# Evacuations of the projections and transposes raised in priority, the seeds' work on g one slot later

## The chip, the cores and the metric

The kernel runs on one core of a Trainium2 chip. A core has a matrix engine (PE, with its weight loads listed as PEld), a vector engine (DVE), an activation engine (ACT), a general engine (POOL) and a sync engine (SP) that here only issues DMA transfers. Each engine executes its own instruction list strictly in order and waits on semaphores for the others. The metric is the device time of one execution in microseconds (us), as the median of several runs.

## The reference

Two independent halves, joined on the last axis. The first is a state-space convolution over 2048 positions and 448 channels with 256 complex states per channel; the second is a 16-head softmax attention over 2048 positions, 28 values per head.

```python
A = -jnp.exp(log_A_real) + 1j * A_imag
C = (C_real + 1j * C_imag) * dt[:, None]
P = jnp.exp((A * dt[:, None])[:, :, None] * pos[None, None, :])
K = 2.0 * jnp.einsum("dn,dnl->dl", C, P).real
y = irfft(rfft(u) * rfft(K)) + u * D_skip

q, k, v = split(x @ wqkv)
o = softmax(q @ k.T * scale) @ v
b = o @ wo
return concatenate([y, b], axis=-1)
```

## The kernel before

The kernel has an opening and a main loop. In the opening, x is transposed on PE and multiplied with the split weights (48 projection jobs, 12 matmuls each); the results go to DRAM and are read back in the layout that attention needs. Next to that the "seeds" of the convolution are computed: eight groups `o` of channels, each of which produces the powers and phases (tiles `tri`, `sg`, `qhat`) from which the main loop later builds the kernel K. In the main loop the scores, exponentials and products with v run on PE and ACT, and the convolution fills the other engines. At the end of the opening the row maxima of the first query block are computed (tiles `p` and `rl`, 16 rounds), negated into `mh`, and sent by two small DMAs into `qhat`; the first score matmul (`pss`) waits for these.

What sets the order of the work differs between the two parts. In the main loop the instructions stay in the order in which the code issues them. In the opening a scheduler orders each engine's list: every instruction carries a priority that follows from the place at which the code issues it, and of those that it takes to be ready, the scheduler puts the one with the earliest place first. A buffer is given out again when the instructions that use it are done.

The opening's code is written in slots. `slots[t]` holds the seeds' steps that fall into slot t, and `project()` is called between slots so that the 48 jobs spread over the first 37 of 41 slots. A seeds group o starts its step list at slot 4·o; the steps are named in the list that `seeds` returns. Those that matter here:

- `times_dt` and `exp_a` (ACT, tile `nat`) prepare a group's inputs; `turn` transposes them on PE into a PSUM tile `pn` (8 matmuls `pn<-ident,nat`) and copies one part on ACT (`tr`).
- `phases` multiplies on POOL (`tri<-tr,pw`) and on DVE (`tri<-pn,pw` and two more of 1680 elements, the last of them in `reduce`).
- `sines` and `sizes` are ACT work on `tri` and `sg` with sine and exponential tables; a change between these needs a table load (`ACT_TABLE_LOAD`).
- `factors`, `g_base` and `e_all` are POOL multiplications (`sg<-sg`, `tri<-tri`, `qhat<-tri`); `g_base` also has a copy of 224 elements on ACT.
- `g_first` is nine DVE operations on `sg` and a PSUM tile `px` of which there is one; `g_copies` is four ACT copies (`sg<-pn`, `sg<-px`); `put_e` and `put_g` are the stores of `qhat` and `sg`.

A job's result is a PSUM tile `pm`, of which there are three. The next use of a `pm` tile waits for the evacuation of the job three before. The evacuation of a K or Q job is an ACT copy and a DVE subtraction into `hl` (two buffers, stored by DMA), for some K jobs also `kb` and `dhl`; that of a V job one ACT copy into `v`. `project()` issues the matmuls of one job and then the evacuation of the job before, which waits in the list `pend`. `transposes(c)` does the same for x: four PE transposes into `pt`, one ACT copy `xh`, one DVE subtraction `xl`.

When the opening's PSUM pools are closed, four `p` tiles of two banks each take over all eight banks: the first two tiles lie over the `pm` banks and one `pt`, the next two over the other `pt`, the two `pn` and `px`. In the code order, all seeds' steps stand ahead of the maxima.

All helpers record through line 76, so the profile shows line 76 everywhere and the tile names tell what an instruction is. In this document job n is the n-th projection job (0 to 47; 40 to 47 are the last K and Q jobs), and a tile with a number, such as `pn6` or `sg7`, is that tile of seeds group 6 or 7 (0 to 7).

Of the kernel before, what the change touches and what calls it, by code (L numbers as in the profile page):

```python
# [8 lines left out]
F32 = mybir.dt.float32  # L9
F32R = mybir.dt.float32r  # L10
I32 = mybir.dt.int32
AF = mybir.ActivationFunctionType
ALU = mybir.AluOpType
# [28 lines left out]
SGB, XB, XL = 2, 5, 4  # L42
K0, KP, KD, UP = 0, 3.5, 4, 3
A0, A1, KW = 26, 34, (33, 35, 36)

N1 = 32
N2 = 64
# [44 lines left out]
def body(ctx, tc, a, out):  # L92
    nc = Engines(tc)
# [119 lines left out]
    with ExitStack() as st:  # L213
# [100 lines left out]
        def seeds(o):  # L314
# [105 lines left out]
            put_e = lambda: nc.sync.dma_start(sd_d[o][:, :, :F_G].rearrange("b p f -> p b f"), q["se"])  # L420
            put_g = lambda: nc.sync.dma_start(sd_d[o][:, :, F_G:].rearrange("b p f -> p b f"), q["sg"])

            def load():
                if o not in nats:
# [1 line left out]
                q["nat"] = nats.pop(o)  # L426
            dts = lambda *r: [lambda i=i: times_dt(i) for i in r]
            return [[load], dts(1, 2, 3), [], [exp_a] + dts(0), [turn, phases], [g_place, reduce], [sines], [sizes, places, g_base],
                    [e_all, g_first], [put_e, factors], [g_copies], [], [put_g]]

        xh, xl = {}, {}

        def transposes(c):
            for k in range(NCK):
                pt = ps_t.tile([128, CQ], F32, name="pt")[:CK]
                for t in range(4):
                    nc.tensor.transpose(pt[:, t * 128:(t + 1) * 128], xns[c, t // 2][:, t % 2, k * CK:(k + 1) * CK], ident)
                xh[k] = x_p.tile([CK, CQ], F32R, name="xh", bufs=XB)
                xl[k] = x_p.tile([CK, CQ], F32R, name="xl", bufs=XL)
                nc.scalar.activation(xh[k], pt, AF.Copy)  # L440
                nc.vector.tensor_tensor(xl[k], pt, xh[k].bitcast(F32), ALU.subtract)

        def qk_proj(c, s, g):
            pp = w_tile()
# [46 lines left out]
        for c in range(NQ):  # L491
            jobs = [lambda c=c, s=s, g=g: qk_proj(c, s, g) for g in range(G) for s in (1, 0)]
            v_jobs = [lambda c=c, t=t: v_proj(c, t) for t in range(4)]
            jobs = v_jobs + jobs if c == NQ - 1 else jobs + v_jobs
            jobs[0] = (lambda c, f: lambda: (transposes(c), f())[1])(c, jobs[0])
            if c + 1 < NQ:
                jobs[1] = (lambda c, f: lambda: (load_x(c + 1), f())[1])(c, jobs[1])
            work += jobs
        stages = [seeds(o) for o in range(NO)]
        n_stage = SP * (NO - 1) + len(stages[0])  # L500
        slots = [[] for _ in range(n_stage)]
# [4 lines left out]
        pend, n_work = [], len(work)  # L506
# [10 lines left out]
        def project():  # L517

            e = work.pop(0)() if work else None
            while pend:  # L520
                pend.pop(0)()
            if e:
                pend.append(e)

        for t in range(n_stage):
            while work and n_work - len(work) < n_work * (t + 1) / PW:
                project()
            for f in slots[t] + ahead.get(t, []):
                f()
            if t + 1 == PW:  # L530
                project()
                wst.close()
                load_k(0, HG - 1, k0_p)
                load_q(1)
                for c in range(NQ):
                    load_v(0, c)
# [211 lines left out]
    def fin(u, s_):  # L748
# [15 lines left out]
        def scale():  # L764
            pw = w_tile()
            for t in range(4):
                nc.tensor.transpose(pw[:, t * 128:(t + 1) * 128], rb[:, t].rearrange("p h e -> p (h e)"), ident)
            nc.vector.tensor_tensor(on, o, pw, ALU.mult)
            if g < G - 1:
                nc.sync.dma_start(on_d[c][g], on)  # L770
            else:
                p_due.extend((s_ + PD + PS * t, lambda t=t: project(t)) for t in range(4))
# [385 lines left out]
```

## Time and profile before

| | |
|---|---|
| median of 3 runs | 1303.45 us (1303.38 to 1304.3) |
| the profiled execution, its own time | 1307.74 us |
| its span | 1305.7 us |
| first score matmul `pss` in it | 242.89 us after the span's start |
| PE busy over the span | 1228.7 us (94%) |
| ACT, DVE, POOL busy over the span | 980.3, 907.0 and 865.9 us |

The page splits the span into 40 slices of 32.6 us; the opening is the first seven and a half. There PE's row reads 6, 8 and 7 tenths, behind it mostly 9. A row of a timeline reads: start, duration, engine, line, operation, output<-inputs, shapes, count, and in brackets how long the engine sat idle before it and what ended the wait. A row of waits reads: who waited for whom, us in total, times, longest. The chain of waits is followed back from the end of a stretch, step by step, to what released each instruction.

### The profile page before, as it was taken

The numbers are of one execution on the slowest core, as the hardware profiler recorded it, in microseconds if no ns is written. First come the engines' busy times: TensorE is split into PE (matmuls) and PEld (weight loads), VectorE is DVE, ScalarE is ACT, GpSimd is POOL, SyncE is SP. The second block draws the span as 40 slices with busy tenths as digits, with TensorE's granted clock in tenths as the row PEclk, the third lists the DMA queues.
The fourth block names the chain that finished last, engine by engine and source line by source line (L and its number), as shares of the span: only waits on it lengthen the run. The fifth ranks groups of instructions, "written<-read, shape, count | busy, mean of one in ns | idle before, by whom it ended". The sixth has DMA issues, their size and how long they took to land.

```text
span 1305.7 us, 32148 instructions
## 1 busy us (share of the span) xinstructions
PE 1228.7 (94%) x12193; PEld 695.7 (53%) x12193; DVE 907.0 (69%) x2001; ACT 980.3 (75%) x2046; POOL 865.9 (66%) x684
## 2 busy tenths in 40 slices
PE   6888877799999999999999999999997999999998
PEld 5766755355555555555555555555554555545333
DVE  5676656677777787777788888888986555636111
ACT  4877875588888888888788888888886666756463
POOL 2677654478888788888769999999995221424421
PEclk9989887799999999999999999999999999999999
DMA  6677679735866455468634232743324453647666
GB/s 202 207 273 257 218 259 271 212 66 136 185 147 142 109 149 157 142 169 231 162 104 105 56 83 62 157 111 78 82 59 139 146 158 136 203 142 238 202 161 175
DMA packets 200082, 205.28 MB, mean 157 GB/s; under 512 B 95992, under 2 KB 158520, under 8 KB 197880
## 3 DMA queue, kind: packets, MB, share of 16 engines
q1 hardware_dynamic: 199864, 203.22, 56.1%
q8 instruction: 96, 1.57, 0.5%
q14 instruction: 58, 0.48, 0.1%
q10 hardware_dynamic: 64, 0.02, 0.0%
HBM read 120.74 MB, written 82.18 MB: 155 GB/s over the span
## 4 chain that ended last, share of the span: by engine, by line
PE 72%; POOL 8%; ACT 7%; DVE 5%; DMA 4%; issue 4%; SPq 0%; ACTq 0%; POOLq 0%
PE pm L76 39%; PE pss L76 16%; PE po L76 16%; POOL sg L76 2%; POOL e L76 2%; DMA khat<-k 2%; POOL tri L76 2%; ACT tri L76 1%; ACT sg L76 1%; DVE mx L76 1%; POOL p L76 1%; ACT L76 1%; ACT p L76 1%; POOL eu L76 1%; DVE rl L76 1%
## 5 line engine op out<-in xcount | busy, mean ns | idle before, releaser
L76 ACT ACTIVATE p<-pss 128x512 f32<-128x512 f32 x1024 | 560.4, 609 | 109.9 <-PE pss L76 105.9
L76 PE MATMUL pss<-qhat,khat 128*128 128x512 f32 x1024 | 405.7, 402 | 4.0 <-DMA qhat<-mh 2.2
L76 DVE TENSOR_REDUCE mx<-pm 128x1 f32<-128x512 f32 x480 | 308.3, 683 | 121.2 <-PE pm L76 119.5
L76 PE MATMUL pm<-khat,qhat 128*128 128x512 f32 x720 | 314.4, 437 | 6.1 <-ACT rl L76 3.5
L76 POOL TENSOR_TENSOR e<-e,sdb 128x256 f32<-128x256 f32 x168 | 202.0, 1203 | 108.7 <-ACT e L76 67.2
L76 PE MATMUL po<-p,v 128*32 128x512 f32 x2048 | 271.0, 597 | 0.0
L76 POOL TENSOR_TENSOR e<-e,eu 128x256 f32<-128x256 f32 x168 | 248.3, 1478 | 13.2
L76 PEld LDWEIGHTS pm<-khat,qhat 128*128 128x128 f32 x720 | 135.4, 188 | 206.4 <-ACT p L76 47.0
L76 PEld LDWEIGHTS pss<-qhat,khat 128*128 128x128 f32 x1024 | 191.2, 189 | 52.5 <-ACT p L76 13.8
L76 DVE CUSTOM_DVE_ANT_0 rl<-pm,rl 128x512 f32<-128x512 f32 x240 | 165.3, 689 | 70.0 <-ACT rl L76 67.7
L76 POOL TENSOR_TENSOR eu<-e,sdb 128x256 f32<-128x256 f32 x168 | 202.3, 1204 | 0.0
L76 POOL TENSOR_TENSOR p<-pr,pr 64x448 f32<-64x448 f32 x64 | 73.2, 1144 | 155.6 <-PE pm L76 122.3
L76 DVE TENSOR_TENSOR g<-g,zg 128x128 f32<-128x128 f32 x392 | 162.0, 413 | 3.6
L76 ACT ACTIVATE rl<-pm 128x512 f32<-128x512 f32 x240 | 145.3, 605 | 7.7 <-issue 4.1
L76 PE MATMUL pm<-xh,khat 112*128 112x512 f32 x256 | 89.7, 431 | 19.6 <-DVE hl L76 10.6
L76 PE MATMUL pm<-kdif,qhat 128*128 128x512 f32 x240 | 97.0, 404 | 1.7 <-DVE pr L76 1.1
L76 DVE TENSOR_TENSOR zg<-g,zg 128x128 f32<-128x128 f32 x224 | 88.0, 393 | 5.3
L76 PEld LDWEIGHTS pm<-e,g 128*32 128x32 f32 x3584 | 56.9, 110 | 49.2 <-issue 15.7
L76 PE MATMUL pm<-e,g 128*32 128x64 f32 x3584 | 73.6, 223 | 8.7 <-POOL e L76 8.7
L76 ACT ACTIVATE y<-pm 128x448 f32<-128x448 f32 x48 | 26.5, 553 | 59.7 <-PE pm L76 39.1
L76 PEld LDWEIGHTS pm<-xh,khat 112*128 112x128 f32 x256 | 51.0, 205 | 35.9 <-DVE hl L76 12.6
L76 DVE TENSOR_TENSOR pr<-pm,ub 128x448 f32<-128x448 f32 x64 | 37.0, 619 | 46.9 <-PE pm L76 37.7
(133 smaller groups left out, 1491.6 us busy)
## 6 DMA issues: line engine op xcount, KB each, us to landing
sdb<-sd SPq DMA_DIRECT2D x56, 336.0 KB
khat<-k SPq DMA_DIRECT2D x64, 256.0 KB
qhat<-q SPq DMA_DIRECT2D x64, 256.0 KB
sd<-sg SPq DMA_DIRECT2D x8, 1456.0 KB
k<-hl SPq DMA_DIRECT2D x16, 512.0 KB
q<-hl SPq DMA_DIRECT2D x16, 512.0 KB
v<-v SPq DMA_DIRECT2D x32, 256.0 KB
mw<-in_mw SPq DMA_DIRECT2D x16, 512.0 KB
```

Of the source, the lines that this page charges most:

```text
L76: i = f(*args, **kw)
```

## The change

Three places are edited, all in the opening.

```diff
+PRI = 200
...
             return [[load], dts(1, 2, 3), [], [exp_a] + dts(0), [turn, phases], [g_place, reduce], [sines], [sizes, places, g_base],
-                    [e_all, g_first], [put_e, factors], [g_copies], [], [put_g]]
+                    [e_all], [put_e, factors, g_first], [], [g_copies], [put_g]]
...
-                nc.scalar.activation(xh[k], pt, AF.Copy)
-                nc.vector.tensor_tensor(xl[k], pt, xh[k].bitcast(F32), ALU.subtract)
+                with tc.high_priority(offset=PRI):
+                    nc.scalar.activation(xh[k], pt, AF.Copy)
+                    nc.vector.tensor_tensor(xl[k], pt, xh[k].bitcast(F32), ALU.subtract)
...
-            while pend:
-                pend.pop(0)()
+            with tc.high_priority(offset=PRI):
+                while pend:
+                    pend.pop(0)()
```

Within `tc.high_priority(offset=PRI)` an instruction is ranked as if it had been issued 200 places earlier. This covers the evacuations of all 48 jobs with the DMA stores that they issue, and the two evacuation steps of all 16 x tiles. The seeds' `g_first` moves from step 8 to step 9 of a group's list and `g_copies` from step 10 to step 11. `put_g` stays in step 12, so that its slot is the old one. No instruction is added or removed: the lists of the engines hold the same instructions before and after, in another order up to the maxima of the first block, and in the same order from there on.

## The prediction

> **What bounds the kernel now.** The change reorders the opening alone, so I read the opening, from the chain of waits that ends at the first score matmul. Of it (start, duration, what):
>
> ```profile
> 200.78 0.63 POOL tri L76
> ...
> 205.06 0.56 DVE sg L76
> ...
> 205.80 0.40 ACT sg L76
> ...
> 206.69 0.76 DVE hl L76
> ...
> 218.32 10.46 DMA khat<-k
> ...
> 236.38 5.56 DMA qhat<-mh
> 242.00 2.99 DMA sdb<-sd
> ```
>
> The seeds' last group finishes its copies at 206.2 (I call this the seeds' end), the last K evacuation follows at 206.69, the khat loads wait for that evacuation's store in SP's list, the maxima wait for khat, and `mh` takes 5.56 us to land. PE's timeline gives the two instants that I measure by: the transposes `pn6` of group 6, and the first score.
>
> ```profile
> 159.05 0.71 PE L76 MATMUL pn<-ident,nat 56*128 56x56 f32 x8
> ...
> 242.89 0.77 PE L76 MATMUL pss<-qhat,khat 128*128 128x512 f32 x1 [2.18 <-DMA qhat<-mh]
> ```
>
> From 242.89 on PE is nearly saturated, and the main loop's order does not change. I therefore count each us by which the first score moves as one us of the total. Now PE's waits between 28 and 177 us, the stretch from job 4 to the start of job 44, and its work there (first pair behind the times: PE busy; then PEld, DVE, ACT, POOL, clock, DMA share, GB/s):
>
> ```profile
> PE pm L76 <- ACT v L76: 6.3, 5, 3.1
> PE pm L76 <- DVE hl L76: 6.2, 4, 2.0
> PE pm L76 <- DVE kb L76: 3.9, 3, 1.7
> PE pt L76 <- DVE xl L76: 1.9, 1, 1.9
> PE pm L76 <- ACT xh L76: 0.8, 1, 0.8
> ```
>
> ```profile
> 28.00:177.00 149.00, 129.85 (x590) 103.18 (x589) 101.67 (x149) 115.22 (x204) 98.12 (x68) 0.94 0.72 242
> ...
> 190.00:240.00 50.00, 34.20 (x111) 22.99 (x110) 27.51 (x50) 29.39 (x37) 15.50 (x12) 0.80 1.05 290
> ```
>
> All of PE's idle time there, 6.3 + 6.2 + 3.9 + 1.9 + 0.8 = 19.1 us, ends with an evacuation. These are exactly the instructions that are raised. The second window shows the DMA engines full from 190 to 240.
>
> **The change part by part.** Nothing is added or removed, 17 table loads included; what counts is which list position each thing gets. In the new lists an evacuation stands right behind its job on ACT and DVE. The seeds fall back against the jobs: `pn6` stood within job 38 on PE and now stands within job 44, behind 7 of its matmuls; `pn7` stood behind job 41 and now stands behind job 45. On ACT the last Q evacuation moves from the 254th to the 233rd place, while the last copy of group 7 moves only from the 252nd to the 254th. So the seeds' tail, from `pn6` to the seeds' end, now lies mostly behind the projections. I cost it in four steps.
>
> *When pn6 runs.* Before it PE has to do what it did up to 177, less the two `pn` groups (2 x 0.7 us), plus 7 matmuls of job 44 (about 1.6 us): 129.85 + 0.2 us of work from 28 us on, so 158.1 us if no idle time is left and 177.2 if all 19.1 us stay or are replaced. Replacement is possible: PE can now wait in the middle of a job for `nat`, which ACT prepares with lower rank, or for an `hl` buffer whose store has not landed. I take a quarter as left, 5 us, because every one of the five rows is of a raised instruction: 163. Both ends are kept.
>
> *From pn6 to the seeds' end.* The durations (count | us in total, mean ns of one):
>
> ```profile
> L76 ACT ACT_TABLE_LOAD x17 | 21.8, 1283 | 1.0 <-PEq L1148 0.7
> L76 ACT ACTIVATE tri<-tri 128x1008 f32<-128x1008 f32 x16 | 16.7, 1043 | 10.7 <-POOL tri L76 10.7
> L76 ACT ACTIVATE tri<-tri 128x1680 f32<-128x1680 f32 x8 | 12.8, 1604 | 0.0
> L76 ACT ACTIVATE sg<-tri 128x672 f32<-128x672 f32 x16 | 12.2, 764 | 3.8 <-POOL tri L76 3.7
> L76 ACT ACTIVATE hl<-pm,kones 128x512 fp32r<-128x512 f32 x16 | 10.9, 679 | 3.7 <-DMA k<-hl 2.4 <-PE pm L76 1.3
> L76 ACT ACTIVATE tri<-tri,half_pi 128x1008 f32<-128x1008 f32 x8 | 9.1, 1136 | 0.0
> L76 ACT ACTIVATE sg<-tri,half_pi 128x672 f32<-128x672 f32 x8 | 6.8, 853 | 0.0
> ```
>
> ```profile
> L76 POOL TENSOR_TENSOR qhat<-tri 128x784 f32<-128x784 f32 x16 | 29.8, 1869 | 0.0
> L76 POOL TENSOR_TENSOR sg<-sg 128x672 f32<-128x672 f32 x16 | 27.5, 1722 | 24.6 <-ACT sg L76 21.4 <-DVE pn L76 3.0
> L76 POOL TENSOR_TENSOR tri<-tr,pw 128x1680 f32<-128x1680 f32 x8 | 24.1, 3006 | 17.4 <-ACT tr L76 11.6 <-issue 5.8
> L76 POOL TENSOR_SCALAR sg<-sg 128x672 f32<-128x672 f32 x8 | 16.7, 2090 | 0.6
> L76 POOL TENSOR_TENSOR tri<-tri 128x224 f32<-128x224 f32 x16 | 10.7, 670 | 17.0 <-ACT tri L76 16.9
> ```
>
> I follow the new order from `pn6` at 0. POOL's 3.0 us product of group 6 ends at 4.2. ACT's exponential (1.04) and the last scaling for group 7 (about 0.5) end at 5.9; `pn7` runs; POOL's product of group 7 ends at 10.2. ACT: exponential of 7 to 11.3, two evacuations (about 0.65 each) to 12.6, table load to 13.9, sines of 6 (0.76 + 1.04) to 15.7, absolute value (about 1.5 net of overlap) to 17.2, cosine into `sg6` to 18.1, the last evacuation and the other cosine to 19.8. POOL in its order has one `sg6` product, a `tri6` and a 1.87 us `qhat6` ahead, until 18.9; then 1.72 + 2.09 + 0.67 to 23.4. The nine operations of `g_first` took from 201.4 (end of the first quoted chain row) to 205.6, 4.2 us; so to 27.6, and the copies, some 0.8, to 28.4. ACT is held by those copies, and only then does group 7: sine 0.76, load 1.28, exponential 0.76, absolute value 1.6, load 1.28, cosine 0.85, to 34.9. POOL 1.72 + 2.09 + 0.67 to 39.4, `g_first` to 43.6, copies to 44.4. Before it was 206.2 - 159.05 = 47.1 us, with six more evacuations and the waits that they brought in between. The seeds' end so falls at 163 + 44.4 = 207.4, about 1 us later than now.
>
> The Trainium skill bears on this step. DVE's last product of 1680 elements took 4.36 us once, beside a POOL product:
>
> ```profile
> 126.54 4.36 DVE L76 TENSOR_TENSOR tri<-tri 128x1680 f32<-128x1680 f32 x1
> ```
>
> ```profile
> 126.13 3.00 POOL L76 TENSOR_TENSOR tri<-tr,pw 128x1680 f32<-128x1680 f32 x1 [2.45 <-ACT tr L76]
> ```
>
> By the Trainium skill ("SBUF — State Buffer", Who interferes with whom), a DVE operation with two SBUF inputs and a GpSimd operation that reads SBUF shut each other out, and the second waits for the whole of the first; the trace agrees, since 1.9 us behind 129.13 is 131.0 and the row ends at 130.9. In the new tail that product of group 7 would meet POOL's group 6 products and push them back by some 1.9 us; by the rule my sum below would be 1298 instead of 1296.
>
> *From the seeds' end to the first score.* Now (rows of POOL, then of ACT):
>
> ```profile
> 207.42 5.86 POOL L76 TENSOR_SCALAR nq<-qhat 128x512 fp32r<-128x512 f32 x4 [2.16 <-DMA qhat<-q]
> ```
>
> ```profile
> 211.73 1.94 ACT L76 ACTIVATE rl<-p 128x1024 f32<-128x1024 f32 x2 [4.59 <-PE p L76]
> ...
> 229.66 2.18 ACT L76 ACTIVATE rl<-p 128x1024 f32<-128x1024 f32 x2 [1.82 <-PE p L76]
> ```
>
> The first `rl` came 5.5 us behind the seeds' end, because `nq` waited for a `qhat` load and PE for the last evacuation; and one round waited 1.82 us for khat. From the first `rl` to the issue of `mh` it took 236.38 - 211.73 = 24.65 us. After the change the last evacuation is some 24 us ahead of the seeds' end, so `qhat` and khat have landed. The first `rl` then waits for POOL, which has to finish the last `qhat` products (0.4 + 3.7 us behind 39.4) and one `nq` of 1.5 us: 1.4 us behind the seeds' end. Without the khat wait `mh` is issued 22.8 us later, at 231.6. The stores of group 7 no longer stand before it in the DMA engines; I take the 2.99 us of the `sdb` load as its landing, and 0.95 us from landing to the score as now (242.89 - 241.94): 235.5. If that cover fails, the old 5.56 costs 2.6 us more.
>
> *The DMA engines.* SP's list now has the khat loads behind the last Q store. Behind it stand 0.5 MB for that store, six `kdif` pieces of 0.06 MB, and by these rows 16 khat, 8 qhat and 2 `sg` stores of groups 5 and 6 and one of group 7; three v loads of 0.26 MB and two `qhat` stores of some 0.9 MB complete it.
>
> ```profile
> khat<-k SPq DMA_DIRECT2D x64, 256.0 KB
> qhat<-q SPq DMA_DIRECT2D x64, 256.0 KB
> ...
> sd<-sg SPq DMA_DIRECT2D x8, 1456.0 KB
> ```
>
> That is about 14 MB, at the 290 GB/s of the window 48 us. The Q store would go out at 163 + 20.5 = 183.5, so the DMA engines are done at 231.7, about when `mh` is issued. They set the same end, and bar a much earlier one.
>
> The moved `g_first` and `g_copies` cost nothing by themselves: their list places in the tail are in the walk above; without that cover each slot they move would cost one slot's work at most, some 4 us, once. Sum: 242.9 - 235.5 = 7.4 us less. The profiled execution's own time is 1307.74, 4.3 us above the median of 1303.45; I take the gain off the median: 1303.45 - 7.4 = 1296.0.
>
> **The rivals.** (1) *The seeds are held by PE* (slower). `pn6` and `pn7` now stand behind six and four more jobs. For: PE must do 130 us of work before `pn6`, and of 28 to 177 only 19.1 us can go. The total of the later steps is 44.4 + 1.4 + 22.8 + 3.0 + 0.95 = 72.5 us, so the change loses as soon as `pn6` starts behind 170.4, that is when over 12.3 of the 19.1 us stay. With all of it replaced, `pn6` at 177.2 gives a first score at 249.7: 1310. Against: all five wait rows name raised instructions. (2) *No change*: the gain on the projections is eaten by the longer tail, `pn6` between 168 and 173; 1303. (3) *More than I take*: no idle time left and the ACT waits on POOL's products (14.4 us in the two rows above, 10.7 + 3.7) shrink too, since groups 2 to 6 now have 5 to 11 instructions between `tr` and the exponential where four of them had 1 to 4. For: that order is in the new lists. Against: the DMA engines. `pn6` at 158 gives 1291, with a shorter walk 1286.
>
> That the ranks do nothing is excluded: the order on all five lists differs.
>
> **How the numbers follow.** Faster by between 2.6 and 12 us, my forecast: 0.44. More than that: 0.12. Within 0.2% (2.6 us, about what a measurement of this kernel can tell from no change): 0.13. Slower by the first rival: 0.31. So faster 0.56, same 0.13, slower 0.31. The range goes from the low end of (3), less 0.05 left out, 1287, to the full price of (1), 1310; the forecast's own is 1291 to 1300.
>
> **What would show it.** PE's waits for `hl`, `v`, `kb`, `xl` between 28 us and `pn6` fall to about 5 us; `pn6` at 163; last evacuation near 183; the seeds' end near 207; first `rl` 1 to 2 us behind it; `mh` landing in 3 us; first score near 235.5. A `pn6` behind 170, or PE waiting for ACT's `nat`, makes the prediction wrong; so does ACT waiting for PE at evacuations that now stand ahead of the seeds.

## The result, and the profile after

The changed kernel takes 1307.61 us (median of 11 runs, 1305.49 to 1308.47) against 1303.45 us: ratio 1.0025, 95% interval 1.0017 to 1.0032. It is slower by a quarter of a per cent, where 1296 was forecast. The profiled execution's own time is 1307.78 us, 0.17 above its median; its span is 1305.9 us.

The two instants by which the prediction measures, in PE's timeline of the changed kernel (start, duration, instruction, in brackets the idle time before and what ended it):

```profile
159.19 1.22 PE L77 MATMUL pm<-xh,khat 112*128 112x512 f32 x2 [6.21 <-ACT v L77]
...
173.49 0.71 PE L77 MATMUL pn<-ident,nat 56*128 56x56 f32 x8 [1.43 <-ACT nat L77]
...
248.60 0.77 PE L77 MATMUL pss<-qhat,khat 128*128 128x512 f32 x1 [1.97 <-DMA qhat<-mh]
```

`pn6` runs at 173.5 and the first score at 248.6; forecast were 163 and 235.5. PE's waits between 28 and 177 us, and its work in that stretch:

```profile
PE pm L77 <- ACT v L77: 11.6, 4, 6.2
PE pn L77 <- ACT nat L77: 2.2, 2, 1.4
PE pm L77 <- ACT xh L77: 1.9, 1, 1.9
PE pm L77 <- DVE hl L77: 1.9, 1, 1.9
```

```profile
28.00:177.00 149.00, 131.16 (x594) 106.74 (x593) 90.39 (x145) 111.58 (x197) 87.36 (x64) 0.92 0.70 237
```

The waits for `kb` and `xl` are gone and those for `hl` fell from 6.2 to 1.9 us. In their place PE waits 11.6 us instead of 6.3 for V evacuations on ACT, and 2.2 for `nat`. The sum is 17.6 us against 19.1: the idle time was for the most part replaced, as the first rival had it. ACT's timeline shows the longest of these waits:

```profile
152.44 0.39 ACT L77 ACTIVATE tri<-tri 128x224 f32<-128x224 f32 x1 [5.19 <-POOL tri L77]
...
153.63 1.28 ACT L77 ACT_TABLE_LOAD   x1
...
156.64 1.28 ACT L77 ACT_TABLE_LOAD   x1
...
158.61 0.96 ACT L77 ACTIVATE v<-pm 128x448 f32<-128x448 f32 x2
```

The two evacuations at 158.61 are raised, and yet they stand behind a seeds' copy that waits 5.19 us for POOL, and behind two table loads. POOL's own timeline carries the delay one step further: it had waited 8.22 us for a result of ACT (`sg`), and from 142.7 to 152.4, when the copy got its input, it had no idle time to speak of. The row that ends the 8.22 us:

```profile
138.93 1.63 POOL L77 TENSOR_TENSOR sg<-sg 128x672 f32<-128x672 f32 x1 [8.22 <-ACT sg L77]
```

The raise did not take them past these instructions. A likely reason is that the scheduler lists by when it takes an instruction to be ready, and that on the chip the copy ran late; no run tests this.

The end of the chain of waits, and SP's list of DMA issues, first before, then after:

```profile
217.50 1.47 POOL nq L77
...
219.01 21.11 PE p L77 x76
...
243.87 4.59 DMA qhat<-mh
```

```profile
188.73 0.38 SPq L76 DMA_DIRECT2D q<-hl  x1
189.20 0.42 SPq L76 DMA_DIRECT2D sd<-qhat  x1
189.67 2.17 SPq L76 DMA_DIRECT2D kdif<-kd  x2
191.94 2.69 SPq L76 DMA_DIRECT2D khat<-k  x4
195.72 0.39 SPq L76 DMA_DIRECT2D k<-hl  x1
```

```profile
187.46 2.67 SPq L77 DMA_DIRECT2D kdif<-kd  x4
194.74 0.38 SPq L77 DMA_DIRECT2D q<-hl  x1
...
196.72 0.39 SPq L77 DMA_DIRECT2D sd<-sg  x1
...
200.04 0.38 SPq L77 DMA_DIRECT2D sd<-qhat  x1
200.47 2.12 SPq L77 DMA_DIRECT2D kdif<-kd  x2
202.68 2.51 SPq L77 DMA_DIRECT2D khat<-k  x4
```

Before, the first khat loads went out at 191.9, in front of the last K and Q stores. After, the raised stores stand first: the last Q store goes out at 194.7, then come six more `kdif` loads and two stores of the seeds, and khat starts at 202.7. The sixteen rounds are no longer stretched by khat (21.1 us of PE in one row of the chain), but the first `rl` comes at 219.84 instead of 211.73.

### The profile page after: what moved, and what is told of

The parts are those of the page before. It is cut to its first block, busy times and chain, and to the rows that moved or that the text cites. A ratio compares the mean times of both kernels' runs of the same rounds, so it can differ in the third digit from the quotient of the medians.

```text
span 1305.9 us, 32153 instructions
## 1 busy us (share of the span) xinstructions
PE 1219.8 (93%) x12193; PEld 693.3 (53%) x12193; DVE 902.9 (69%) x2001; ACT 982.2 (75%) x2046; POOL 861.7 (66%) x684
## 4 chain that ended last, share of the span: by engine, by line
PE 76%; POOL 8%; DVE 5%; issue 4%; ACT 4%; DMA 2%; SPq 0%; ACTq 0%; POOLq 0%; DVEq 0%
PE pm L77 42%; PE pss L77 16%; PE po L77 16%; POOL sg L77 2%; PE p L77 2%; POOL tri L77 2%; POOL e L77 2%; DMA tri<-in_B_wqkv 1%; DVE mx L77 1%; POOL qhat L77 1%; POOL p L77 1%; ACT p L77 1%; POOL eu L77 1%; DVE tri L77 1%; ACT tri L77 1%
## 5 line engine op out<-in xcount | busy, mean ns | idle before, releaser
L77 PEld LDWEIGHTS pss<-qhat,khat 128*128 128x128 f32 x1024 | 191.2, 189 | 51.9 <-ACT p L77 13.8
L77 PE MATMUL pm<-xh,khat 112*128 112x512 f32 x256 | 89.6, 432 | 12.7 <-ACT v L77 6.2
L77 DVE TENSOR_TENSOR pr<-pm,ub 128x448 f32<-128x448 f32 x64 | 37.0, 620 | 46.3 <-PE pm L77 38.4
L77 PEld LDWEIGHTS po<-p,v 128*32 128x32 f32 x2048 | 54.4, 110 | 26.1 <-issue 21.5
```

The source lines that it names most:

```text
L77: i = f(*args, **kw)
```

## The experiments

All ratios are to the kernel before, run on the same chip beside them; the interval is 95%.

| run | what is in it | median us | ratio | interval |
|---|---|---|---|---|
| the change | steps moved, evacuations and their stores raised | 1307.61 | 1.0025 | 1.0017 to 1.0032 |
| e1 | kernel before | 1303.56 | 0.9997 | 0.9988 to 1.0006 |
| e2 | steps moved only | 1296.43 | 0.9943 | 0.9929 to 0.9957 |
| e3 | raised only | 1304.63 | 1.0010 | 1.0001 to 1.0019 |
| e4 | the change, by 100 instead of 200 | 1302.20 | 0.9987 | 0.9978 to 0.9995 |
| e5 | only `g_first` moved | 1303.70 | 0.9998 | 0.9989 to 1.0006 |
| e6 | only `g_copies` moved | 1293.93 | 0.9929 | 0.9916 to 0.9942 |
| e7 | the change, all seeds' steps raised too | 1312.93 | 1.0070 | 1.0058 to 1.0082 |
| e8 | the change, x evacuations not raised | 1307.88 | 1.0029 | 1.0018 to 1.0040 |
| e9 | the change, stores not raised | 1294.88 | 0.9927 | 0.9914 to 0.9939 |
| e10 | the change, kdif, khat, qhat loads raised | 1317.90 | 1.0107 | 1.0093 to 1.0121 |
| e11 | e6, those loads raised by 50 | 1297.23 | 0.9947 | 0.9935 to 0.9960 |
| e12 | e6, those loads raised by 200 | 1313.97 | 1.0074 | 1.0061 to 1.0086 |
| e13 | the change, `nat` loads raised | 1307.64 | 1.0026 | 1.0016 to 1.0037 |
| e14 | steps moved, only stores raised | 1311.93 | 1.0056 | 1.0044 to 1.0069 |
| e15 | e6, evacuations raised, stores not | 1297.11 | 0.9944 | 0.9932 to 0.9955 |
| e16 | evacuations raised, stores not, no step moved | 1301.02 | 0.9977 | 0.9966 to 0.9989 |
| e17 | the change, `nat` loads and `sd` stores raised | 1315.07 | 1.0087 | 1.0073 to 1.0100 |
| e18 | the change, every DMA of the opening raised | 1308.45 | 1.0035 | 1.0023 to 1.0047 |

**The two parts apart.** e1 is the kernel before again, for a second profile.

> The kernel before once more, to see a second profile of it. Its profiled execution took 1307.74 us where its median is 1303.45; the kernel after was profiled at 1307.78 with a median of 1307.61. Theory A (the opening is what differs between the two kernels): the first score again near 243 us, and the 4 us by which that one execution was long lie behind 243. Rival B (that execution had a slow opening): the first score near 239 in a typical execution. The ratio is 1.000 either way.

The second profile has the first score at 241.0 and an own time of 1305.91 us:

```profile
241.01 0.76 PE L76 MATMUL pss<-qhat,khat 128*128 128x512 f32 x1 [2.16 <-DMA qhat<-mh]
```

In the two profiles of before the span ends 1062.8 and 1062.9 us behind the first score. The 1.8 us between their own times lie in the opening, on rival B's side, as far as two executions can tell.

```diff
e2: without PRI and both high_priority blocks
e3: the list of steps as before:
-                    [e_all], [put_e, factors, g_first], [], [g_copies], [put_g]]
+                    [e_all, g_first], [put_e, factors], [g_copies], [], [put_g]]
e4:
-PRI = 200
+PRI = 100
```

> Only the two seeds' steps on g moved, no raised priority. pn6 stands after 37.5 jobs on PE and pn7 after 43 (before 38.5 and 42, after 44.6 and 46). Theory A (the raised evacuations push the seeds behind the jobs, and that late tail is the loss): pn6 stays near 159, the seeds' end near 206, the time within 1.5 us of 1303.5. Rival B (the moved steps hold the sg and PSUM buffers longer, and that is the loss): seeds' end some 4 us later, 1307.

> Only the raised priority, the seeds' steps in their old slots. pn6 stands after 40.2 jobs, pn7 behind all 48. Theory A: the last seeds group decides, pn7 runs only when the projections are through (near 180 us), so the seeds' end is as late as after or later, 217 to 221, and the time is 1307 to 1311. Rival B (the moved steps are the loss): 1303 or less.

> Both parts, but the evacuations are raised by 100 places and not by 200. pn6 stands after 40.9 jobs, pn7 after 45.1. Theory A: pn6 near 164, pn7 near 178, seeds' end some 2 to 4 us earlier than after, 1304 to 1306. Rival B (the moved steps are the loss): as after, 1307.6.

Neither theory foresaw e2: the moved steps alone gain 7 us. e4 was faster than both theories had it, too: its seeds ended at 209.7, 8.8 us before those of the change. The moved steps' part of the change is not neutral, and the raised priority on top of them costs 1307.6 - 1296.4 = 11.2 us. Without the moved steps it costs 1.3 us (e3, by the ratio). With half the offset it costs 1302.2 - 1296.4 = 5.8 us. In e3 `pn7` ran at 189.0 and the seeds ended at 213.8, earlier than the 217 of theory A, and the time stayed under its 1307.

**Which moved step gains.**

```diff
e5:
-                    [e_all, g_first], [put_e, factors], [g_copies], [], [put_g]]
+                    [e_all], [put_e, factors, g_first], [g_copies], [], [put_g]]
e6:
-                    [e_all, g_first], [put_e, factors], [g_copies], [], [put_g]]
+                    [e_all, g_first], [put_e, factors], [], [g_copies], [put_g]]
```

> Only g_first one slot later, nothing raised, g_copies in the old slot. PE's places are those of before (pn6 after 38.5 jobs, pn7 after 42). The two moved steps together took 1296.4. Theory C (g_first, nine DVE operations that wait for POOL, held evacuations on DVE in its old place): most of the 7 us come from this step, 1297 to 1300. Rival D (the four ACT copies, which wait for DVE, held ACT): this one alone stays at 1302 to 1304.

> Only g_copies one slot later, nothing raised, g_first in the old slot. pn6 stands after 37.5 jobs, pn7 after 43, as with both steps moved. Theory C: 1302 to 1304. Rival D: 1297 to 1300.

It is the copies alone, and with `g_first` left in its slot they gain more: 9.2 us by the ratio, beyond rival D's range. ACT's groups up to 207 us, of e6:

```profile
L76 ACT ACT_TABLE_LOAD x15 | 19.2, 1283 | 1.0 <-PEq L1148 0.7
```

Two of the 17 table loads of before are gone, 2.6 us of ACT. Both are missing in the last stretch: from the copy of `tri` for group 6 (128x224) to the seeds' end it took 25.2 us before (181.0 to 206.2) and 20.8 in e6 (176.0 to 196.9). The rest arises earlier: `pn6` runs at 150.9 instead of 157.2 or 159.0, `pn7` at 167.6, and the last copy ends at 196.9 instead of 204.4 or 206.2. That the copies had held ACT by waiting for DVE, as rival D has it, does not explain this: up to 207 us these waits come to 7.7 us before, to 6.1 in e6, and to 5.0 in e5, which gains nothing. What falls in e6, and does not in e5 (23.7 us), is ACT's wait for POOL's `tri` (28 to 207 us; first before, then e6):

```profile
ACT tri L76 <- POOL tri L76: 21.4, 11, 3.7
```

```profile
ACT tri L76 <- POOL tri L76: 16.6, 9, 3.0
```

This is a reading of three profiles and not a test; why the copies' place brings it stays open. The first score of e6:

```profile
234.28 0.77 PE L76 MATMUL pss<-qhat,khat 128*128 128x512 f32 x1 [2.29 <-DMA qhat<-mh]
```

**What in the raised priority costs.** The first thought was that the seeds fall back behind the jobs. e7 raises the seeds' steps along with the evacuations; e8 takes the raise off the x evacuations.

```diff
e7: each step of the list that seeds() returns is called within
+                with tc.high_priority(offset=200):
e8: transposes() as before
```

> The kernel after with all of the seeds' steps raised by 200 too, so that evacuations and seeds stand to each other as without any priority, and both ahead of the jobs' matmuls. pn6 stands after 36.4 jobs, pn7 after 41.7. Theory A (what costs in the raised priority is that it puts the seeds behind the jobs): pn6 near 155, the last group's copies done near 204, 1295 to 1300. Rival E (raised evacuations cost by themselves, by the stores that they send earlier or by ACT and DVE waiting for PE at them): 1304 or more.

> Moved steps and only the projections' evacuations raised, those of the transposes not. pn6 stands after 38.2 jobs, pn7 after 43, six and three jobs earlier than in the kernel after. Theory A (the time follows the place of the last seeds groups): close to the moved steps alone, 1295 to 1299. Rival E: close to the kernel after, 1305 to 1308.

e7 is a miss for theory A. The seeds came early, as it said (`pn6` at 152.9, the last copy at 206.8), and the kernel was the slowest so far: POOL's `nq` began at 225.6 only, because the first `qhat` loads went out at 211.0, behind all raised stores and the seeds' last one. e8 missed it too: `pn6` at 164.4, the seeds' end at 209.8, no faster. Both times are as rival E had them, which named the stores as one way. The engine that sends the stores is SP. There the raised stores are taken back to their old rank in e9, and the loads of `ahead` (`kdif`, khat, `qhat`) are raised along with them in e10.

```diff
e9: in both evac()
-                nc.sync.dma_start(...)
+                with tc.high_priority(offset=-PRI):
+                    nc.sync.dma_start(...)
e10:
-            for f in slots[t] + ahead.get(t, []):
-                f()
+            for f in slots[t]:
+                f()
+            with tc.high_priority(offset=PRI):
+                for f in ahead.get(t, []):
+                    f()
```

> The kernel after, but the DMA stores in the evacuations are not raised, only the ACT and DVE instructions are. On SP the nat loads of groups 6 and 7 and the first khat loads stand again ahead of the last stores, as in the kernel before; pn6 stands after 38.4 jobs, pn7 after 41. Theory F (raised stores in SP's in-order list hold back the loads behind them: nat, and with it the seeds, and kdif and khat; the first score comes some 46 to 51 us behind the first khat load, in every kernel so far): first khat load near 188, 1294 to 1299. Rival E (ACT and DVE waiting for PE at raised evacuations): 1304 to 1308.

> The kernel after, with the loads of kdif, khat and qhat raised by 200 as well, so that they stand among the stores again on SP: eight of the sixteen khat loads ahead of the stores of hl30 and hl31. The seeds stay late (pn6 after 43 jobs, pn7 behind all 48). Theory F: khat starts before 190, and unless the seeds then bound, 1298 to 1302. Theory A (the late seeds alone set the end, as all work on p waits for their last tiles): the seeds' end near 219 as in the kernel after, 1307 to 1311 whatever the loads do.

e9 decides it: with the stores unraised and all else as in the change the kernel takes 1294.88 us. The raised ACT and DVE evacuations cost nothing; the stores that they carry along cost 1307.6 - 1294.9 = 12.7 us. SP in e9:

```profile
185.78 1.98 SPq L77 DMA_DIRECT2D khat<-k  x4
187.86 0.39 SPq L77 DMA_DIRECT2D k<-hl  x1
188.29 1.87 SPq L77 DMA_DIRECT2D qhat<-q  x2
```

Loads and stores alternate again, and khat starts at 185.8 instead of 202.7. `pn6` runs at 154.5. What the order on SP does to the DMA engines is seen between 185 and 195 us. In the change SP stands at the last Q store, which waits until 194.7 for DVE's `hl`, with all khat loads behind it, and the engines' share is 0.36; in e9 it is 0.99 (the last column but one; first the change, then e9):

```profile
185.00:195.00 10.00, 1.35 (x6) 0.75 (x4) 9.61 (x8) 8.08 (x10) 6.72 (x4) 0.69 0.36 131
```

```profile
185.00:195.00 10.00, 5.14 (x22) 3.59 (x20) 5.52 (x11) 6.72 (x16) 5.52 (x4) 0.93 0.99 277
```

From 195 us on the engines are full in both (1.03 and 1.04) until the first score is near, so what was lost before is not made up.

e10 is a miss for both theories: khat started at 178.6, and the time was 1317.9. The seeds were still late (`pn7` at 188.2), and the chain names the store that then held them: with the loads ahead of it the `sg` store took 10.4 us, and ACT's next write to `sg`, of which there are two buffers, waited for it.

```profile
203.92 10.40 DMA sd<-sg
214.35 0.76 ACT sg L77
```

**Loads ahead of stores.** If the start of khat alone set the end, raising the loads in the best kernel should help.

```diff
e11, e12: e6 with the loads of ahead raised as in e10, by 50 or 200
```

> Only g_copies one slot later (1293.9), and the loads of kdif, khat and qhat raised by 50. The lists of POOL, DVE, ACT and PE stay as they are but for a few places; on SP twelve of sixteen khat loads now stand ahead of the stores of hl29 to hl31. Theory F: the first khat load some 6 us earlier than 184.6 and the first score 2 to 6 us earlier, 1288 to 1292. If the seeds' end (196.9) with the sixteen rounds behind it is the bound instead: 1293 to 1295.

> As the run before, but the loads raised by 200: twelve khat loads stand right behind the stores of hl24 and hl25 on SP, near 172. Theory F: as good or better than with 50, 1286 to 1292, until the seeds' end bounds. If loads ahead of the stores hold the stores back (SP waits at a load until the store that it reads has landed, and hl has two buffers): PE waits for hl grow, 1293 to 1298.

It does not. In e11 khat starts at 174.7, ten us earlier than in e6 (184.6), and by the ratios the kernel is 2.3 us slower, with intervals that just overlap. PE's waits (28 to 200 us) for `hl` are longer:

```profile
PE pm L76 <- DVE hl L76: 16.5, 4, 8.2
```

In e6 the same wait is 9.4 us. The longest one ends with an evacuation that ACT began at 196.39, right behind the seeds' last copies. For a store to free an `hl` buffer ACT waited once in the last stretch, 4.0 us, and only behind that, at 201.5. In e12, 20 us slower than e6, it is the V evacuations that PE waits for:

```profile
PE pm L76 <- ACT v L76: 20.9, 6, 10.7
```

The wait of 10.7 us ends with an evacuation at 191.2 that stands on ACT behind the seeds' table loads and copies. SP stood 21.3 us at the V store that needs it, and khat, expected near 172, started at 195.8. So theory F, as I had put it, falls: an early khat is not by itself a gain, and raising the loads by 200 does not even bring it. That loads put ahead hold stores, and these the `hl` buffers and PE, is at most a part of it; by which path they cost is not shown. What is left of the theory is that SP's list is one queue, in which a transfer that waits holds what stands behind it.

**By which transfers the raised stores act.** e13, e17 and e18 raise other transfers beside the stores, e14 raises the stores alone.

```diff
e13:
+                    with tc.high_priority(offset=PRI):
                         load_nat(o)
e14: in both evac() only the nc.sync.dma_start within tc.high_priority(offset=PRI), nothing else raised
e17: e13, and put_e and put_g raised by PRI
e18: e17, and load_x (all but the first) and the loads of ahead raised by PRI
```

> The kernel after with the loads of the seeds' inputs (nat) raised by 200 too, so that they stand again ahead of the stores on SP. pn6 stands after 39.9 jobs instead of 44.6, pn7 after 46.5. If the raised stores cost by holding back nat and with it the seeds: 1297 to 1301. If they cost by holding back kdif and khat: 1304 to 1308.

> Moved steps, and only the stores of the evacuations raised by 200, no ACT or DVE instruction. pn6 stands after 38 jobs and pn7 after 43, as without any priority (1296.4). If raised stores cost by themselves, through kdif and khat behind them on SP: 1302 to 1308. If they cost only where the seeds fall back behind the jobs with them: 1295 to 1298.

> The kernel after with the seeds' loads (nat) and stores (sd) raised by 200 too; on SP all sixteen khat loads still stand behind the last Q store (hl31). pn6 after 38 jobs, pn7 after 45.9. If kdif, khat and qhat behind the raised stores carry the loss: 1303 to 1308. If the seeds' own transfers carry it: 1295 to 1299.

> The kernel after with every DMA of the opening raised by 200, loads and seeds' stores too. On SP khat stands again among the stores of hl26 to hl31, nearly as with the stores unraised (1294.9); pn6 after 38.4 jobs, pn7 after 45. If the order on SP alone carries the loss: 1295 to 1299. If raised transfers cost by something else (pn7 stays 4 jobs late): 1300 to 1305.

e14 shows that raised stores cost by themselves: 1311.9 against 1296.4 with the same steps moved and nothing raised. Its tail, on SP and on POOL:

```profile
207.35 0.38 SPq L77 DMA_DIRECT2D q<-hl  x1
207.78 1.66 SPq L77 DMA_DIRECT2D khat<-k  x3
209.48 1.84 SPq L77 DMA_DIRECT2D qhat<-q  x4
```

```profile
219.14 5.86 POOL L77 TENSOR_SCALAR nq<-qhat 128x512 fp32r<-128x512 f32 x4 [11.29 <-DMA qhat<-q]
```

The seeds ended at 209.9 there, and `nq` then waited 9 us more for a load that stands behind the last Q store. e17 has the same picture (seeds' end 207.6, `nq` at 225.2). In these two, and in e7, the loads behind the raised stores are the bound. In the change itself, in e13 and in e18 the seeds end at 218.5, 216.2 and 214.9 and are the bound, or tie with the loads: in the change the last seeds' products on POOL and the landing of `qhat` (first `p` matmul at 215.7, behind a wait for that load) lie within 2 us of each other. That fits e13, in which `pn6` ran 14 us earlier (159.1) and nothing was gained. e18 leaves a rest: khat stands among the stores again there, nearly as in e9, and still `pn7` runs at 181.4 and the time is 1308.45. In PE's list `pn7` stands behind 45 jobs there, and behind 41 in e9. So the rank of the stores also moves the seeds back in the lists of PE and ACT, and not by way of SP's order alone. Why the scheduler does that is not settled. e10, e12, e14, e17 and e18 all came out slower than every range put on record for them, so the size of these losses is not explained.

**What the raised evacuations are worth.**

```diff
e15: e6 and the raise of e9
e16: the raise of e9, the list of steps as before
```

> Only g_copies one slot later (1293.9) and the ACT and DVE instructions of the evacuations raised, the stores not. With both steps moved the raise was worth 1.5 us (1296.4 to 1294.9); if that adds up: 1292 to 1293. If it is the same gain twice: 1294 to 1296.

> The ACT and DVE instructions of the evacuations raised, no stores raised, the seeds' steps in their old slots: the raise by itself. If it is worth 1.5 us: 1302. If it takes PE's waits for evacuations as the prediction had it: 1296 to 1299. If ACT or DVE waits for PE at them: above 1304.

Alone they gain 3 us (e16, 13 table loads instead of 17). On the moved steps they gain 2 (e9 against e2), on the moved copies alone they lose 2 (e15 against e6); in both pairs the intervals overlap. So the 3 us do not add to the gain of the copies. e6 and e9 are the fastest of all, 0.7% below the kernel before, and their intervals all but coincide.

## Why the prediction was wrong

**When `pn6` runs: the step that failed.** The prediction let a quarter of the 19.1 us of PE's idle time stand, 5 us; 17.6 us stood, in part with other owners. `pn6` came at 173.5 and not at 163, 10.5 of the 13.1 us by which the first score was late against the forecast. (Its own sum gives 175.7 with 17.6 us of idle time; PE's work before `pn6` was 127.7 us and not 130.05.) The text had named the break-even (170.4), the first rival, and ACT's `nat` as a thing to wait for; it failed in taking five rows of raised instructions as a reason that the waits would go. Such rows show who ended a wait, not what that instruction had stood behind. In the longest wait it was the seeds' copy on ACT that waits for POOL, and that stayed ahead. The waits do not go with the stores unraised either: PE's idle time up to 177 us is 17.4 us in e9 and 19.9 in e16. `pn6` is early in e9 (154.5) because it stands behind 38.4 jobs on PE and not behind 44.6. By the rival's own chain (72.5 us from `pn6` on) 173.5 gives a first score at 246.0 and 1306.6 us; measured were 248.6 and 1307.61. The chain adds up for this kernel, but an early `pn6` alone would not have saved it: in e13 it ran at 159.1, `pn7` only at 183.7, and the time was the same.

**The stores.** The text costed the raised stores only as bandwidth, within 14 MB from 183.5 on. It did see that khat moves behind the last Q store, and its DMA bound had the right length: from that store to the issue of `mh` it took 48.4 us (194.74 to 243.17, DMA share 1.02) where 48 were forecast. But the store went out 11.2 us later than the 183.5 taken, about as late as `pn6`, and the text gave no price to what waits behind it. e9 gives the price of the raised stores as a whole: unraised stores would have made the forecast true within 1.1 us (1294.9 against 1296.0), though by another sum, since 7 of those 8.6 us come from the moved steps.

**The moved steps.** "Cost nothing by themselves" was wrong in sign and size: they gain 7 us, all from the copies. The text looked for cover for their work, and not for what the copies' place in ACT's list does to the work around them: moved alone, they leave 15 table loads of 17, and ACT's waits for POOL's `tri` are 4.8 us shorter (e6). The 17 loads, rightly found equal in the two kernels, hid a part of it. e9 has 15 again, but so have e13, e14, e17 and e18 with raised stores, so these two loads are not what the stores cost.

**From `pn6` to the seeds' end.** The walk along the lists gave 44.4 us; it took 218.5 - 173.5 = 45.0. The sum was right within 0.6 at its end and within 1.4 on the way: group 6's products on POOL ended 24.7 us behind `pn6` (23.4 forecast), its copies 29.5 (28.4), group 7's cosine 35.8 (34.9) and its products 40.1 (39.4). The rows of the seeds' end, of the first `rl` and of `mh`:

```profile
217.93 0.56 ACT L77 ACTIVATE sg<-px 128x112 f32<-128x112 f32 x2 [1.54 <-DVE sg L77]
219.84 1.02 ACT L77 ACTIVATE rl<-p 128x1024 f32<-128x1024 f32 x1 [1.36 <-PE p L77]
...
243.17 1.24 ACTq L77 DMA_DIRECT2D qhat<-mh  x2
```

**From there to the first score.** The first `rl` 1.3 us behind the seeds' end (1.4 forecast), the issue of `mh` 23.3 us later (22.8 forecast), both right. `mh` landed at 248.46, 5.3 us behind its first issue, where I took 3.0 because the stores of group 7 would not stand before it. They did: SP issued them at 236.5 and 237.8, behind its v loads, and the DMA engines were full (share 1.06 from 235 to 245 us). That these held `mh` up is likely, and not tested apart. This term was 2.3 us too small, and the old 5.56 that the text named as the other end was nearer. The score then came 0.1 us behind the landing, where 0.95 was taken.

**DVE and POOL in the tail.** Here the rule quoted in the prediction came true. DVE's last product of group 7 and POOL's product of group 6, from the two timelines of the changed kernel:

```profile
191.12 2.99 DVE L77 TENSOR_TENSOR tri<-tri 128x1680 f32<-128x1680 f32 x1
```

```profile
190.50 1.84 POOL L77 TENSOR_TENSOR qhat<-tri 128x784 f32<-128x784 f32 x1
192.30 3.30 POOL L77 TENSOR_TENSOR sg<-sg 128x672 f32<-128x672 f32 x1
```

DVE's row ends 1.8 us behind POOL's `qhat` product, and POOL's next product takes 3.30 instead of 1.64 us, ending 1.5 us behind DVE. By the Trainium skill ("SBUF — State Buffer", Who interferes with whom) each waits for the whole of the other; the trace agrees, with 1.7 us for POOL's product where the prediction expected some 1.9.

**One us of the first score is one us of the total: too simple by 5.7 us here.** The first score came 5.7 us later than in the profile of before, or 7.6 later than in the second one; the own times differ by 0.0 and 1.9. Part of it is a second wait in that place. ACT's first exponential stands behind `e`, which needs an `sdb` load; first before, then after:

```profile
245.15 0.63 ACT L76 ACTIVATE e<-sdb 128x256 f32<-128x256 f32 x1 [6.02 <-DMA sdb<-sd]
...
246.36 1.08 ACT L76 ACTIVATE p<-pss 128x512 f32<-128x512 f32 x2
```

```profile
248.19 0.63 ACT L77 ACTIVATE e<-sdb 128x256 f32<-128x256 f32 x1 [3.14 <-DMA sdb<-sd]
...
249.41 0.59 ACT L77 ACTIVATE p<-pss 128x512 f32<-128x512 f32 x1
```

Before, `sdb` kept the exponentials from starting for 3.5 us behind the first score; after, 0.8. The first exponential is thus only 3.05 us later. From there to the end of the span it took 1059.3 us before and 1056.5 after; where these 2.8 us of the main loop come from stays open.

## What to carry to other kernels

A priority put around a block of code raises the DMAs in it too, and on an in-order issue list a raised store that waits for its data holds every load behind it: raise the evacuation, and look at each queue that its transfer passes (here 12.7 us). A row of waits names the instruction that ended them, so before taking such a wait as curable, read on that engine what the instruction stood behind. When a change has two parts, measure each alone: here one gained 7 us, and the other gave back 11.

## What the runs showed of the hardware

PE's pace falls behind a shorter wait than expected. Behind the 6.21 us wait the twelve matmuls of one job took 5.50 us in the chain, at a granted clock of 0.50 from 159.2 to 164.5; undisturbed ones follow each other every 0.23 us, 2.8 for a job, at a clock of 1.00 (166 to 172 us). The same is seen after the 1.43 us wait ahead of `pn6`: from 175.2 to 178.2 the matmuls of the next job followed each other every 0.43 us, at a clock of 0.50. That stretch begins 1.7 us behind the wait, with eight small transposes in between, so that the wait brought it is inferred. In the kernel before, the clock is 0.50 from 131.61 to 134.3, right behind a wait of 1.87 us.

```profile
159.19 5.50 PE pm L77 x12
```

```profile
175.20 0.63 PE L77 MATMUL pm<-xl,khat 112*128 112x512 f32 x1
175.63 1.05 PE L77 MATMUL pm<-xh,khat 112*128 112x512 f32 x2
176.48 0.63 PE L77 MATMUL pm<-xl,khat 112*128 112x512 f32 x1
```

The Trainium skill ("TensorE: Matmul & The Clock Gate", Part 1: The HAM clock gate) puts the fall to half pace behind an idle window of some 3.4 us. The trace agrees for the long wait; behind the two shorter ones, of 1.43 and 1.87 us, it shows the same half pace.
